# Earlier transposes for chunk 4, a new head order and a later first output step in a retention plus maxout-FFN kernel

## The chip, the cores and the metric

The kernel runs on one core of one Trainium2 chip. A time is the device time in microseconds (us) of one execution. Each kernel was executed several times, and a profile was taken of one of those executions. The profile gives every instruction's start and duration, what ended the idle time before it, and the clock that was granted to TensorE (PE). PE does the matmuls, VectorE (DVE) and ScalarE (ACT) work element by element, GpSimd (POOL) helps them, and SyncE (SP) issues nearly all the transfers. Where two kernels are compared by a ratio, they ran on the same chip in the same rounds.

## The reference

A retention layer (attention with a decaying causal mask) feeds a feed-forward layer (FFN) with a maximum over three products:

```python
B, H, S, D = 8, 8, 576, 64                      # q, k, v: float32
scores = scale * q @ k.transpose(0, 1, 3, 2)
Dmat   = where(rel >= 0, gamma[h] ** rel, 0)    # rel = query position - key position
attn   = (scores * Dmat) @ v
x = attn.transpose(0, 2, 1, 3).reshape(4608, 512)
h = maximum(maximum(x @ w1, x @ w2), x @ w3)    # w1, w2, w3: 512 x 768, float64
out = h @ w_out                                 # w_out: 768 x 512
```

## The kernel before

The rows are cut into 36 chunks of 128. Retention works chunk by chunk with a running state per head. Four chunks make one FFN tile of 512 rows, so there are nine tiles. The retention of tile t+1 is interleaved with the FFN of tile t. Only tile 0 has nothing to hide its four chunks behind, and it also has to convert the float64 weights ("pieces" of 128 columns) as they arrive. This change is about that start.

The order of program at the top is this. On PE, instructions run in this order, and each other engine also takes its own in the order written:

```python
    warm(6)                          # 6 identity matmuls, so that PE's clock is up
    for g in range(CPT):             # CPT = 4 chunks in a tile
        load(g)                      # k, q, v of chunk g
        ...
    load_weights(2)
    load(CPT)                        # chunk 4
    load_weights(4)
    decay_values(0); transposes(0)
    ...                              # gq on ACT's queue (see the diff)
    warm(2)
    scores(0); transposes(1); decay_values(1); state(0)
    values([0], [0])
    keep(0); scores(1); transposes(2); decay_values(2); state(1); keep(1)
    values([1], [1])
    transposes(3); decay_values(3); scores(2)
    convert(2)                       # weight piece 0 on DVE and ACT
    scores(3); state(2); keep(2)
    convert(2)
    values([2], [2])
    convert(2)                       # first half of weight piece 1
    decay_values(4)
    values([3], [3])
    keep(3)
    transposes(4)
    convert(4)
    # then tile 0's FFN, with the rest of chunk 4 inside it
```

Chunks are transposed on PE and copied out of PSUM by ACT. Chunk 4 still uses the two-buffer pool `ps_x`, whose banks the first FFN matmuls use as well:

```python
        for n, src in (("k", raws["k", g]), ("q", raws.pop(("q", g)))):
            pool, tag = (ps_r, "r") if g > CPT else (ps_x, "x")
            pt = pool.tile([P, NP, C], FP32, tag=tag, name=n + "t")
            for p in range(NP):
                nc.tensor.transpose(pt[:, p, :], pair(src, p), ident[:C, :C])
            t = both[n] = att.tile(...)
            nc.scalar.copy(t[:], pt[:])
```

The heads are laid out in the FFN's input so that block n holds head n in its upper 64 rows and, in its lower 64, a head of the other four with neighbours swapped. The weights' rows have to be loaded in that order, which takes three loads a piece:

```python
    def head(c, n):
        return NP * c + (n ^ c)                        # half c of block n; NP = 4
    ...
            for c, n in ((0, slice(0, NP)), (1, slice(0, NP, 2)), (1, slice(1, NP, 2))):
                h = slice(0, NP) if c == 0 else slice(head(c, n.start), H, 2)
                nc.sync.dma_start(blocks[half(c), n], heads[:, h])
```

`values` ends with the output step of its chunks: two DVE multiplications of PSUM by `gq`, which give the FFN's input `xT`.

## Time and profile before

| kernel before | |
|---|---|
| median of 3 runs | 799.44 us (799.01 to 800.44) |
| profiled execution: span, mean clock | 798.8 us, 0.998 |
| PE busy | 787.9 us |
| first FFN matmul starts | 29.12 us |
| span less that start | 769.7 us |

One view is to be added: SP's queue in the timeline of the kernel before (start, duration, instruction, how many in a row). SP issues loads one after the other, so the time in this queue delays every load behind it.

```profile
14.12 5.30 SPq L314 DMA_DIRECT2D bits<-in_moe_w_dram  x6
19.52 1.27 SPq L164 DMA_DIRECT2D kraw<-in_k_dram  x2
```

The first two weight pieces are six loads and hold the queue for 5.3 us. Chunk 4's k (two loads, since the chunk crosses from one batch to the next) is issued at 19.52.

### The profile page before, as it was taken

How to read it: one execution, taken by the hardware profiler on the slowest of the kernel's cores; microseconds unless marked ns; L12 is line 12 of the kernel's file. 1: busy time of each engine (PE TensorE's matmuls, PEld its weight loads, DVE VectorE, ACT ScalarE, POOL GpSimd, SP SyncE). 2: the span in 40 equal slices, each digit the busy share in tenths (PEclk: the TensorE clock that was granted, in tenths of full speed). 3: DMA queues.
4: the chain of work that ended last, by engine and by line, in shares of the span. 5: the costliest groups of instructions: out<-in, count | busy, mean ns of one | idle time of the engine just before them, and what ended most of it. 6: DMA issues, size and time to landing. Idle time of an engine off the chain costs nothing. (4 is left out here: it accounts for less than half of the span.)

```text
span 798.8 us, 13706 instructions
## 1 busy us (share of the span) xinstructions
PE 787.9 (99%) x5128; PEld 643.5 (81%) x5128; DVE 415.2 (52%) x833; ACT 174.4 (22%) x402; POOL 140.1 (18%) x158
## 2 busy tenths in 40 slices
PE   8899999999999999999999999999999999999998
PEld 6545546888888888888888888888888888888887
DVE  2997978664354634363535344544545343642341
ACT  3654642111111102111111111111111121111211
POOL 2210107421210130112211121112111201110000
PEclk9999999999999999999999999999999999999999
DMA  9995643333333332332233333333333323001001
GB/s 214 225 229 119 162 107 101 56 57 58 88 57 56 57 78 49 75 59 60 61 55 57 65 84 57 55 58 89 58 56 57 78 56 64 1 14 41 1 1 53
DMA packets 237506, 59.27 MB, mean 74 GB/s; under 512 B 218240, under 2 KB 236160, under 8 KB 237440
## 3 DMA queue, kind: packets, MB, share of 16 engines
q1 hardware_dynamic: 236720, 58.14, 33.5%
q8 instruction: 40, 0.66, 0.4%
q10 hardware_dynamic: 720, 0.27, 0.1%
q14 instruction: 26, 0.21, 0.1%
HBM read 48.89 MB, written 9.44 MB: 73 GB/s over the span
## 5 line engine op out<-in xcount | busy, mean ns | idle before, releaser
L498 PE MATMUL x<-S,T 128*128 128x256 f32 x576 | 148.2, 380 | 1.2 <-ACT p L503 1.2
L498 PEld LDWEIGHTS x<-S,T 128*128 128x128 f32 x576 | 108.8, 190 | 17.7 <-ACT p L503 2.8
L348 POOL TENSOR_TENSOR H<-h 128x256 f32<-128x256 f32 x24 | 21.0, 874 | 321.5 <-DVE h L541 321.5
L498 PE MATMUL x<-xT,w 128*128 128x256 f32 x288 | 76.1, 387 | 0.0
L498 PE MATMUL x<-S,w 128*128 128x256 f32 x288 | 74.4, 381 | 0.4 <-DVE h L528 0.4
L498 PE MATMUL z<-xT,T 128*128 128x256 f32 x288 | 74.0, 379 | 0.0
L498 PE MATMUL y<-xT,w 128*128 128x256 f32 x288 | 73.9, 379 | 0.0
L498 PE MATMUL z<-S,w 128*128 128x256 f32 x288 | 73.9, 379 | 0.0
L528 DVE TENSOR_TENSOR tmp<-x,p 128x256 f32<-128x256 f32 x48 | 20.4, 425 | 100.2 <-PE x L498 100.2
L269 DVE TENSOR_TENSOR xT<-o,gq 128x512 f32<-128x512 f32 (+1 forms) x40 | 23.7, 632 | 87.7 <-PE o L262 84.0
L503 ACT COPY p<-x 128x256 f32<-128x256 f32 x72 | 26.9, 373 | 191.7 <-PE x L498 191.7
L560 PE MATMUL up<-xT,w 128*128 128x512 f32 x144 | 65.2, 609 | 2.6 <-ACT kT L188 2.6
L498 PEld LDWEIGHTS z<-xT,T 128*128 128x128 f32 x288 | 54.2, 189 | 8.2 <-ACT p L503 0.3
L498 PEld LDWEIGHTS y<-xT,w 128*128 128x128 f32 x288 | 54.7, 190 | 7.4
L498 PEld LDWEIGHTS z<-S,w 128*128 128x128 f32 x288 | 54.7, 190 | 7.4
L498 PEld LDWEIGHTS x<-xT,w 128*128 128x128 f32 x288 | 53.0, 190 | 9.6 <-issue 1.5
L498 PEld LDWEIGHTS x<-S,w 128*128 128x128 f32 x288 | 49.4, 189 | 13.8 <-issue 1.3
L560 PEld LDWEIGHTS up<-xT,w 128*128 128x128 f32 x144 | 27.4, 194 | 35.5 <-issue 30.2
L227 POOL TENSOR_TENSOR state<-state,gs 128x256 f32<-128x256 f32 x24 | 20.1, 837 | 179.2 <-DVE state L226 179.2
L199 DVE TENSOR_TENSOR st<-s,causal 128x512 f32<-128x512 f32 x72 | 45.0, 684 | 11.6 <-PE s L196 10.7
L168 POOL TENSOR_TENSOR vd<-vraw,gk 128x512 f32<-128x512 f32 x36 | 38.6, 1074 | 64.8 <-DMA vraw<-in_v_dram 64.8
L503 ACT COPY u<-x 128x256 f32<-128x256 f32 x72 | 26.8, 373 | 99.5 <-PE x L498 88.6
(93 smaller groups left out, 1086.0 us busy)
## 6 DMA issues: line engine op xcount, KB each, us to landing
out_dram<-osb SPq DMA_DIRECT2D x35, 256.0 KB, 2.1
kraw<-in_k_dram SPq DMA_DIRECT2D x32, 256.0 KB, 3.1
vraw<-in_v_dram SPq DMA_DIRECT2D x32, 256.0 KB, 3.5
qraw<-in_q_dram SPq DMA_DIRECT2D x464, 16.0 KB, 1.9
kxraw<-in_k_dram SPq DMA_DIRECT2D x464, 16.0 KB, 1.9
bits<-in_moe_w_dram SPq DMA_DIRECT2D x18, 256.0 KB, 4.4
bits<-in_moe_w_dram SPq DMA_DIRECT2D x36, 128.0 KB, 4.2
bits<-in_moe_w_out_dram SPq DMA_DIRECT2D x6, 512.0 KB, 4.9
```

The costliest lines, as they stand in the source:

```text
L168: nc.gpsimd.tensor_tensor(t[:], raws.pop(("v", g))[:], gk[:].unsqueeze(2).to_broadcast([C, H, D]), op=ALU.mult)
L199: nc.vector.tensor_tensor(st[:, j], s[j][:], masks[start_of(g)][:].unsqueeze(1).to_broadcast([C, NP, C]), op=ALU.mult)
L227: nc.gpsimd.tensor_tensor(t[:], t[:], gs[:], op=ALU.mult)
L269: nc.vector.tensor_tensor(xT[t][:, b::2, i * C:(i + len(chunks)) * C].rearrange("p u (m c) -> p u m c", c=C), o[b][:].rearrange("p m u c - ...
L348: chores.append(lambda: (pool(s3, a11, a21, op=ALU.subtract), pool(s4, a12, s2, op=ALU.subtract)))
L498: nc.tensor.matmul(out[:], lhsT=w[:, d * P:(d + 1) * P], rhs=xS[t][n][:, d, :], start=first and d == 0, stop=d == 1, skip_group_check=True)
L503: nc.scalar.copy(c[:], src[:])
L528: nc.vector.tensor_tensor(c22, x[:], p7[:], op=ALU.add)
L560: nc.tensor.matmul(ps[:], lhsT=w_sb[i, fb][:, dc * P:(dc + 1) * P], rhs=xT[t][:, dc, :], start=(dc == 0), stop=(dc == NDC - 1))
```

## The change

Its intent is to take chunk 4's transposes out of the gap before the first FFN matmul, and to shorten what comes before. There are five parts:

1. `transposes(4)` moves ahead of the second weight piece and of chunk 3's values, and takes its PSUM buffers from the four-buffer pool `ps_r`.
2. Head 4c + n goes to half c of block n, so that a weight piece takes two loads instead of three, and `gq` two instead of four. The tiles of the state product now come in another order.
3. Chunk 0's output step runs after chunk 1's scores.
4. Two of six warm-up matmuls become 24 quarter-array ones (a matmul is two instructions here, so 4 instructions become 48).
5. The state update at the end of `values` now comes after the code that sums `xT` for later tiles, as a result of splitting the function.

```diff
-    gq = const.tile([P, NP, C], FP32, name="gq")
+    gq = const.tile([P, 2, NP // 2, C], FP32, name="gq")
@@
+    def warm_quarters(n):
+        ps = [ps_y.tile([P, P // 2], FP32, tag="y", name="warm") for _ in range(2)]
+        for _ in range(n):
+            for r in range(2):
+                rows = ident[P // 2 * r:P // 2 * (r + 1), :P // 2]
+                for c in range(2):
+                    nc.tensor.matmul(ps[r][P // 2 * c:P // 2 * (c + 1), :], lhsT=rows, rhs=rows, start=True, stop=True)
@@ transposes
-            pool, tag = (ps_r, "r") if g > CPT else (ps_x, "x")
+            pool, tag = (ps_r, "r") if g >= CPT else (ps_x, "x")
@@ head
-        return NP * c + (n ^ c)
+        return NP * c + n
@@ values: its end becomes a function of its own
+        finish = partial(output, chunks, o, t, i)
+        if later:
+            return finish
+        finish()
+        for g in new_states[:1]:
+            if g >= CPT:
+                keep(g)
+
+    def output(chunks, o, t, i):
         if i == 0:
             xT[t] = xpool.tile([P, NDC, NT], FP32, tag="xT", name="xT")
         ...
-        for g in new_states[:1]:
-            if g >= CPT:
-                keep(g)
         ... (sums of xT for tiles after the first)
@@ load_weights
-                for c, n in ((0, slice(0, NP)), (1, slice(0, NP, 2)), (1, slice(1, NP, 2))):
-                    h = slice(0, NP) if c == 0 else slice(head(c, n.start), H, 2)
-                    nc.sync.dma_start(blocks[half(c), n], heads[:, h])
+                for c in range(2):
+                    nc.sync.dma_start(blocks[half(c)], heads[:, head(c, 0):head(c, NP)])
@@ top
-    warm(6)
+    warm(4)
+    warm_quarters(6)
@@
-        for b in range(2):
-            nc.scalar.dma_start(gq[half(c), b::2, :], out_decay[half(b ^ c), NP // 2 * c:NP // 2 * (c + 1), :])
+        of_rows = out_decay[:, NP // 2 * c:NP // 2 * (c + 1), :].rearrange("(b p) u c -> p b (u c)", b=2)
+        nc.scalar.dma_start(gq[half(c)].rearrange("p b u c -> p b (u c)"), of_rows)
@@
-    values([0], [0])
+    first_output = values([0], [0], later=True)
     keep(0)
     scores(1)
+    first_output()
@@
     values([2], [2])
+    transposes(4)
     convert(2)
     decay_values(4)
     values([3], [3])
     keep(3)
-    transposes(4)
     convert(4)
```

(The changed reading of `gq` in the output step is cut.)

## The prediction

> **What bounds the kernel now.** I read the page first, then the timeline of each engine over the first 45 us, then the windows view, then the waits.
>
> The page's busy table says that TensorE (PE) fills the span:
>
> ```profile
> PE 787.9 (99%) x5128; PEld 643.5 (81%) x5128; DVE 415.2 (52%) x833; ACT 174.4 (22%) x402; POOL 140.1 (18%) x158
> ```
>
> The chain that ended last contains nothing but matmuls back to about 724 us, and the windows view has PE busy for all of 30 to 100 us and of 150 to 300 us. So after the first large matmul the run is a fixed queue of matmuls, and the change can only act on when that queue starts, how fast it runs, and the cost of the attention matmuls in it. Of the span less busy time, 798.8 - 787.9 = 10.9 us, 1.44 is before the first matmul and about 2.9 after the last one (795.9). About 4 us more lies between 5 and 30 us, where this change works. The PE timeline there (start, duration, instruction, in brackets the idle time before it and what ended it):
>
> ```profile
> 22.91 1.42 PE L249 MATMUL o<-st,vd 128*64 128x128 f32 x15
> ...
> 24.87 0.67 PE L262 MATMUL o<-qT,state 64*64 64x128 f32 x16
> 25.47 0.66 PE L186 MATMUL kt<-ident,kraw 128*128 128x128 f32 x4
> 25.96 0.60 PE L186 MATMUL qt<-ident,qraw 128*128 128x128 f32 x4
> 29.12 8.83 PE L560 MATMUL up<-xT,w 128*128 128x512 f32 x16 [2.56 <-ACT kT L188]
> ...
> 47.43 7.03 PE L560 MATMUL up<-xT,w 128*128 128x512 f32 x16
> ```
>
> PE finishes chunk 4's transposes at 26.56, idles 2.56 us, then starts the feed-forward. Its first 16 matmuls take 8.83 us where the same 16 take 7.03 us at 47 us: 1.80 us lost. The windows view (busy per engine, then PEclk, the DMA share, GB/s) shows why:
>
> ```profile
> 26.29:29.70 3.41, 0.85 (x5) 0.37 (x4) 3.41 (x8) 2.40 (x4) 1.57 (x2) 1.00 0.81 226
> 29.70:33.11 3.41, 3.41 (x6) 1.33 (x5) 3.38 (x8) 1.74 (x3) 0.75 (x1) 0.50 0.94 254
> ```
>
> The clock is 0.50 for exactly 3.41 us, after 3.41 us in which PE was busy 0.85. Half of 3.41 is 1.7 us, which agrees with the 1.80. So the gap costs 2.56 us of idleness and 1.8 us of clock.
>
> What ended the gap was ACT's copy of chunk 4's kT out of the bank that the first feed-forward matmul reuses. ACT could not make it earlier, since its FIFO had the second weight piece's activations first, and those wait for DVE:
>
> ```profile
> 27.12 0.72 ACT L437 ACTIVATE expo<-expo,top 128x512 f32<-128x512 int32 x1 [2.95 <-DVE expo L434]
> 27.88 0.72 ACT L440 ACTIVATE expo<-expo,inf 128x512 int32<-128x512 f32 x1
> 28.50 0.56 ACT L188 COPY kT<-kt 128x512 f32<-128x512 f32 x1
> ```
>
> DVE is the second limit. It has no idle time from 19.95 to 37.7 us:
>
> ```profile
> 19.95 1.29 DVE L199 TENSOR_TENSOR st<-s,causal 128x512 f32<-128x512 f32 x2 [2.07 <-PE s L196]
> 21.33 0.43 DVE L434 TENSOR_SCALAR expo<-bits 128x512 int32<-128x512 int32 x1
> ...
> 27.00 1.27 DVE L439 TENSOR_SCALAR frac<-bits 128x512 int32<-128x512 int32 x1
> 28.19 0.74 DVE L269 TENSOR_TENSOR xT<-o,gq 128x256 f32<-128x256 f32 x2
> ...
> 31.04 0.69 DVE L456 TENSOR_TENSOR w<-mant,expo 128x512 f32<-128x512 f32 x1
> ```
>
> The line at 28.19 is chunk 3's output step, whose first half ends near 28.6; the first feed-forward matmul needs it. So the kT copy (ends 29.06) hides a second wait only 0.4 to 0.5 us shorter.
>
> **What the Trainium skill says.** (1) "TensorE: Matmul & The Clock Gate", Part 1: PE's clock passes half its pulses after an idle window and all after a busy one; the window is about 3.4 us and free-running. The trace agrees on the 3.41 us and the half rate. It differs on the trigger: a gap of 2.56 us, shorter than a window, was enough, with PE busy 0.85 of 3.41. (2) Same page, Part 3: matmuls in different row and column tiles of the array run side by side. The trace agrees: 32 of the 64x64 tiles (L262, N=128) take 1.03 us from their start at 119.89 to the next group's at 120.92, 32 ns each, against some 107 for a whole-array instruction of that N (0.43 us at N=512, over 4). (3) "SBUF — State Buffer", Who interferes with whom: DVE's two-input and two-port instructions and GpSimd block one another. The trace agrees: the frac above took 1.27 us beside a GpSimd multiply at 26.77, and 0.42 elsewhere. (4) "DMA: Bandwidth & Descriptors", Issuing engines are not separate DMA queues: several issuers only save issue time. Here issue time is itself something: three loads per weight piece take 0.65 us each on SP where nothing blocks them.
>
> **The change, part by part.**
>
> *Chunk 4's transposes* move ahead of the second piece and of chunk 3's values, into the four-bank pool. ACT copies kT and qT before it takes up the second piece, and the first feed-forward matmul's bank was read long ago. The wait that remains is DVE's chunk 3 output; DVE's own order does not change, so its first half still ends near 28.6. Direct gain: 29.12 - 28.65 = 0.45 us.
>
> The rest of the gap is filled by moving chunk 3's values (about 2.5 us: 22.91 to 25.47) behind the transposes. These need k4 and q4, which SP issues from 19.52 to 22.15 now. I expect kt at 23 and qt at about 24.2, hence values 3 from 24.7 to 27.0, and a gap of 28.4 - 27.0 = 1.4 us in place of 2.56. The window from 26.29 would then be busy 0.7 + 1.3 = 2.0 of 3.41, 58%. It throttled at 25%; it did not in the windows from 9.23 (2.46 busy, 72%) and 12.64 (81%). I give 75% that the clock stays up, a gain of 1.75 us.
>
> *Head order 4c + n.* Loads per weight piece go from 3 to 2, those of gq from 4 to 2. In the timeline six piece loads sit between 14.12 and 19.42 on SP, 0.88 us each, ahead of chunk 4's loads; two fewer bring k4, q4 and v4 some 1.3 to 1.8 us forward, which is what makes the transposes possible at 23 us. The bytes are the same and the DMA share is near 1.0 until 17 us, so q3 (18.2) and the first piece's bits (21.3), which start DVE's chain, move little: estimate 0.3 us earlier. On ACT, gq's issue takes 4.12 us (6.04 to 10.16) and holds back kT of chunk 1; half of that goes. But chunk 3's q, on which PE waits until 18.20, absorbs it.
>
> On PE the tiles of L262 now come as r0c0, r0c1, r1c0, r1c1 and each bank gets one row half. Column pairs of the same rows already overlap (L249: 32 in 1.79 us, 56 ns each, half of 107), and so do row pairs (L196: 32 in 1.98 us). L262 is at 32 ns, a quarter of 107 plus a fixed 0.16 us per group, so there is nothing to win there: 0.
>
> *Chunk 0's output later.* DVE waited 2.58 and 1.16 us for gq and held back chunk 1's mask. That wait now lies behind chunk 1's scores. Chunk 1 comes about 1.5 us earlier and runs into the same wait for q3: 0.
>
> *Warm-up.* Four full matmuls fewer (4 instructions, 0.24 us each at the cold clock) and 24 quarter tiles more (48 instructions). At four abreast, N=64, cold, an estimate is 48 x 107 / 4 = 1.3 us plus a drain. So chunk 0 starts perhaps 0.5 us later, which the slack of about 2 us before q3 takes up: 0.
>
> Sum: 0.45 + 0.3 + 0.75 x 1.75 = 2.1 us; with a little for loads that arrive better than I assume, 2.4.
>
> Does it carry to the end? The closest pieces in the first feed-forward: the second is ready at 31.73 and its matmul would start at 28.4 + 3.43 = 31.8 (tight, perhaps 0.1 lost); later pieces are ready 2.5 us or more before use, and DVE idles for PE at 39, 51, 55 and 66 us, so it moves with PE. Yes, nearly all.
>
> **Rivals.** (a) *The clock still falls*: the free-running window may lie otherwise, and a gap of 1.4 us may be enough. Then only 0.5 to 0.9 us comes: 798.6. Chance a quarter. (b) *DVE becomes the bound*: v4 lands earlier, so GpSimd's multiply meets another DVE instruction and may lengthen the chain by up to 0.8 us; the tight second piece would wait too. About 798. (c) *q4 comes late*: since PE is in order, transposes ahead of values 3 hold those back past 28 us; then the new wait is for q4: 799 to 800. The early issue speaks against it. (d) *The new tile order loses overlap*: at two abreast L262 would gain 0.43 us per 16, over 448/16 = 28 groups 12 us: 810. The overlap of column pairs seen in L249 speaks against it: 4%. (e) *The transfers come earlier than I think* and DVE's chain with them: 795.5.
>
> **Range and chances.** From the median 799.44, less 2.4: 797.0. The runs before spread over 1.4 us, and the clock is worth 1.8; so 795.3 to 799.2. Two per cent is 16 us, which nothing in the first 30 us can give. Slower by 2% needs (d) and more: 0.02; faster: 0.01.
>
> **What would show it.** First feed-forward matmul at 28.0 to 28.7, released by DVE's xT of L269 and no longer by ACT; PEclk 1.00 from 30 to 33 and 16 such matmuls in 7.0 us; kt and qt of chunk 4 ahead of the last values; SP's k4 issue near 18; L262 still near 32 ns. I am wrong if the clock still dips, if PE waits for q4, or if L262's busy time grows.

## The result, and the profile after

| | before | after |
|---|---|---|
| median | 799.77 us (799.01 to 800.44, 4 runs) | 798.75 us (797.69 to 799.21, 4 runs) |
| span and clock of the profiled execution | 798.8 us, 0.998 | 796.0 us, 1.000 |
| first FFN matmul starts | 29.12 us | 28.75 us |

The ratio of after to before is 0.9986, with a 95% interval of 0.9968 to 1.0003: the same within 2%, and about 1.1 us less. Here and below a ratio is the mean time of one kernel's fast runs over the mean time of the other's fast runs of the same rounds. That is not quite the ratio of the medians quoted.

The profiled execution of after was its luckiest. It was the 797.69 one, and its clock stayed at 1.000. The other three had 0.997 or 0.998 and took 798.53 to 799.21 us. So the traces show 2.8 us between the kernels where the medians show 1.0.

The busy table of after:

```profile
PE 785.0 (99%) x5172; PEld 643.0 (81%) x5172; DVE 417.6 (52%) x833; ACT 174.4 (22%) x402; POOL 139.9 (18%) x158
```

PE has 44 instructions more (48 of quarter matmuls for 4 of full ones) and is busy 2.9 us less, though the work is the same. Most of that is clock: 1.7 us in the first 16 FFN matmuls, as the next view shows. PE's timeline of after (start, duration, instruction, in brackets the idle time before it and what ended it):

```profile
21.26 0.67 PE L270 MATMUL o<-qT,state 64*64 64x128 f32 x16
24.67 0.63 PE L194 MATMUL kt<-ident,kraw 128*128 128x128 f32 x4 [2.74 <-DMA kraw<-in_k_dram]
25.52 0.63 PE L194 MATMUL qt<-ident,qraw 128*128 128x128 f32 x4 [0.22 <-issue]
26.08 1.09 PE L257 MATMUL o<-st,vd 128*64 128x128 f32 x16
...
27.57 0.67 PE L270 MATMUL o<-qT,state 64*64 64x128 f32 x16
28.75 7.13 PE L573 MATMUL up<-xT,w 128*128 128x512 f32 x16 [0.51 <-DVE xT L286]
```

The gap in front of the FFN has shrunk from 2.56 to 0.51 us, and its releaser is now DVE instead of ACT. But a new gap of 2.74 us has opened four us earlier, where the transposes wait for chunk 4's k. The FFN starts 0.37 us earlier. Its first 16 matmuls now last 7.06 us from their start to the next group's (28.75 to 35.81), where before had 8.76 (29.12 to 37.88). The two add up to 0.37 + 1.70 = 2.07 us at that point. The difference stays there, at 2.04 to 2.07 us, up to about 479 us. The trace of before then shows a few more stalls of 0.2 to 0.45 us each, which have no counterpart in the change.

What DVE and ACT did at the same place in after (two answers of the timeline, one for each engine):

```profile
28.27 0.76 DVE L286 TENSOR_TENSOR xT<-o,gq 128x256 f32<-128x256 f32 x2 [1.05 <-PE o L270]
```

```profile
25.34 0.59 ACT L196 COPY kT<-kt 128x512 f32<-128x512 f32 x1 [2.04 <-PE kt L194]
```

ACT's copy is now over long before the FFN. DVE, which had no idle time here before, waits 1.05 us for PE to finish chunk 3's values. So the order of waits is now: transfer of k4, then PE, then DVE, then the FFN. DVE was ready for chunk 3's output at 27.22, earlier than before (28.19), mostly since its instruction at L452 took 0.42 us, where the same one (L439 before) took 1.27 us beside a GpSimd multiply.

SP's queue of after in the timeline:

```profile
14.81 3.03 SPq L327 DMA_DIRECT2D bits<-in_moe_w_dram  x4
17.93 1.27 SPq L172 DMA_DIRECT2D kraw<-in_k_dram  x2
...
21.25 3.08 SPq L172 DMA_DIRECT2D vraw<-in_v_dram  x2
```

k4 is issued 1.59 us earlier than before, as intended. It still lands only at about 24.6, some 6.7 us after its issue.

The new tile order of the state product costs and gains nothing. The groups by form, first before, then after (instructions, then total busy us, mean ns of one, idle before):

```profile
L262 PE MATMUL o<-qT,state 64*64 64x128 f32 x448 | 16.7, 277 | 0.0
```

```profile
L270 PE MATMUL o<-qT,state 64*64 64x128 f32 x448 | 16.7, 277 | 0.0
```

### The profile page after: what moved, and what is told of

Its sections match the earlier page's. It is cut to its first block, busy times and chain, and to the rows that moved or that the text cites. A ratio compares the mean times of both kernels' runs of the same rounds, so it can differ in the third digit from the quotient of the medians.

```text
span 796.0 us, 13774 instructions
## 1 busy us (share of the span) xinstructions
PE 785.0 (99%) x5172; PEld 643.0 (81%) x5172; DVE 417.6 (52%) x833; ACT 174.4 (22%) x402; POOL 139.9 (18%) x158
## 4 chain that ended last, share of the span: by engine, by line
PE 95%; SPq 2%; DMA 1%; issue 0%; ACT 0%; DVE 0%; ACTq 0%
PE x L511 32%; PE z L511 15%; PE dx L383 11%; PE up L573 8%; PE y L511 8%; PE dz L383 5%; PE s L204 4%; PE o L257 4%; PE dy L383 3%; PE down L562 2%; PE o L270 2%; PE kv L224 2%; SPq L172 1%; DMA kraw<-in_k_dram 1%; SPq L327 0%; DMA out_dram<-osb 0%
## 5 line engine op out<-in xcount | busy, mean ns | idle before, releaser
L573 PE MATMUL up<-xT,w 128*128 128x512 f32 x144 | 63.5, 596 | 0.5 <-DVE xT L286 0.5
L383 PE MATMUL dx<-To,H 128*128 128x256 f32 x192 | 44.8, 383 | 0.0
```

Of the source, the lines that this page charges most:

```text
L383: nc.tensor.matmul(out[m], lhsT=hS[n](fp)[:, m * P:(m + 1) * P], rhs=late["T"][n][:, fp, :], start=first and fp == 0 and (m == 0 or last a ...
L573: nc.tensor.matmul(ps[:], lhsT=w_sb[i, fb][:, dc * P:(dc + 1) * P], rhs=xT[t][:, dc, :], start=(dc == 0), stop=(dc == NDC - 1))
```

## The experiments

Twelve kernels were run. A name with `a_` is the kernel after with an edit, one with `b_` the kernel before with an edit. Each was timed in five rounds against the kernel before. "Start" is the start of the first FFN matmul in its trace, "rest" is the span less that start, and "clock kept" counts the runs with a mean clock of 0.999 or more.

| kernel | median us (range) | ratio to before [95%] | start | rest | clock kept |
|---|---|---|---|---|---|
| a_same | 798.14 (796.97–799.80) | 0.9981 [0.9964, 0.9997] | 28.70 | 767.2 | 3 of 6 |
| a_fill | 797.71 (797.30–797.85) | 0.9972 [0.9957, 0.9986] | 28.91 | 767.2 | 5 of 5 |
| b_fill | 798.24 (797.44–800.94) | 0.9987 [0.9969, 1.0005] | 28.96 | 767.1 | 4 of 6 |
| b_transposes | 799.65 (797.65–801.44) | 0.9998 [0.9980, 1.0017] | 27.90 | 768.6 | 3 of 6 |
| b_trans_quarters | 800.05 (798.56–802.30) | 1.0004 [0.9990, 1.0017] | 28.90 | 769.6 | 4 of 6 |
| a_old_heads | 800.01 (798.22–803.20) | 1.0004 [0.9982, 1.0027] | 30.25 | 768.7 | 2 of 6 |
| a_full_warm | 797.88 (796.40–799.05) | 0.9975 [0.9963, 0.9987] | 29.80 | 767.2 | 2 of 5 |
| a_output_first | 798.32 (797.03–799.06) | 0.9976 [0.9961, 0.9991] | 30.08 | 767.2 | 3 of 6 |
| a_k4_early | 796.68 (795.08–797.05) | 0.9956 [0.9943, 0.9969] | 27.74 | 767.3 | 5 of 5 |
| a_k4_osb4 | 797.33 (796.70–797.81) | 0.9965 [0.9951, 0.9980] | 27.89 | 767.3 | 3 of 5 |
| a_k4_osb4_full | 797.29 (796.51–798.59) | 0.9966 [0.9952, 0.9980] | 29.18 | 767.6 | 1 of 6 |
| a_k4_fill | 796.50 (796.32–797.17) | 0.9956 [0.9940, 0.9972] | 26.58 | 768.0 | 6 of 6 |

The kernel before had medians of 799.69 to 800.05. The column "rest" already says much: in seven of the twelve, and in the first profile of after (767.2), it is 767.1 to 767.3, whatever the start. From the first FFN matmul on, the run is a fixed queue. The five others are taken up below.

### The kernel after once more: how much of its gain is the clock

> The changed kernel again, unedited, to see whether its runs fall into two groups. Theory (the granted clock falls or not according to where the free-running 3.4 us window lies against PE's gap of 2.74 us before chunk 4's transposes): runs with a mean clock of 1.000 end near 797.6 us, runs with 0.997 or 0.998 near 799.0 us, about 1.7 us apart. Rival (the spread is noise from elsewhere): times don't follow the clock. Median expected 798.7, ratio to before 0.9985.

This is the unedited kernel after. With the four runs of the first result there are ten runs of it, and 44 of the kernel before from these experiments, so here not all runs are of the same rounds. Sorted by the mean clock of the run:

| | clock 0.999 or more | 0.998 or less | mean of all |
|---|---|---|---|
| before | 5 of 44 runs, mean 798.47 us | 39 runs, mean 800.15 us | 799.96 us |
| after | 4 of 10 runs, mean 797.41 us | 6 runs, mean 799.15 us | 798.45 us |

In either column after is 1.0 to 1.06 us shorter, and in either row a run with a fallen clock is about 1.7 us longer (1.68 and 1.74). The whole difference is 1.50 us. It is the 1.0 us at the same clock, and (39/44 - 6/10) x 1.7 = 0.49 us from falling less often. Ten runs are few to know that share.

### Dummy matmuls in the wait of the kernel after

```diff
+    def fill(n, pool=None, tag="y"):
+        ps = (pool or ps_y).tile([P, P], FP32, tag=tag, name="fillps")
+        for _ in range(n):
+            nc.tensor.matmul(ps[:], lhsT=ident[:], rhs=ident[:], start=True, stop=True)
@@
     values([2], [2])
+    fill(12, ps_x, "x")
     transposes(4)
```

> The changed kernel with 12 idle-time matmuls of the identity (24 instructions, some 2.6 us) put into PE's wait for chunk 4's k, in a bank that nothing else uses then. Theory (the clock): every run keeps a mean clock of 1.000 and ends near 797.5 us, 1.2 us under the median of the changed kernel. Rival (the time is in the wait for k4, or in noise): no change against a_same, clock still 0.997 to 0.998 in some runs.

PE's timeline of this kernel, two groups of it:

```profile
22.15 2.94 PE L134 MATMUL fillps<-ident 128*128 128x128 f32 x24
...
28.91 7.13 PE L578 MATMUL up<-xT,w 128*128 128x512 f32 x16 [0.51 <-DVE xT L291]
```

The dummies lie exactly in the wait for k4 and end about when it has landed. All five runs kept their clock, and they spread over 0.55 us, where the unedited kernel spread over 2.8. The start is no earlier than in the unedited one (28.91 against 28.70), so the whole effect is the clock. As far as five runs can show it, the new wait for k4 is where the kernel after loses its clock.

### The same in the kernel before

```diff
     transposes(4)
+    fill(10)
     convert(4)
```

> The kernel before with 10 idle-time matmuls of the identity (20 instructions, some 2.1 us) in its gap of 2.56 us ahead of the first feed-forward matmul; the wait for ACT's copy of kT stays. Theory (1.8 of the 2.06 us between the two traces are the clock, 0.37 the earlier start): 1.7 us faster than before, near 798.0 us, clock 1.000. Rival (the wait for the copy is what costs): same as before, 799.7.

The profiled run has the first FFN matmul at 28.96 and 16 of them in the time of full clock (7.07 us), and a rest of 767.1. Four of six runs took 797.44 to 798.51. Two took 800.39 and 800.94 at a clock of 0.998, and no trace was taken of those. The profiled run agrees with the account of where the old kernel's 1.7 us went. The whole set is inconclusive: its interval includes 1, and what lowered the clock in two runs isn't known.

### The transposes alone

```diff
-            pool, tag = (ps_r, "r") if g > CPT else (ps_x, "x")
+            pool, tag = (ps_r, "r") if g >= CPT else (ps_x, "x")
@@
     values([2], [2])
+    transposes(4)
     convert(2)
@@
     keep(3)
-    transposes(4)
     convert(4)
```

> The kernel before with only chunk 4's transposes moved ahead and into the other banks; head order, loads and warm-up as before. Theory (PE is in order, so the transposes hold chunk 3's values until k4 and q4 land, and without the earlier issue of the loads these land near 25.5 us): values 3 after 26 us, first feed-forward matmul at 28.7 to 29.5 us, so no earlier start than in the changed kernel, and a gap ahead of the transposes in which the clock can still fall: 799.0 to 800.0 us. Rival (the move alone carries the gain): 798.7.

PE's timeline of this kernel:

```profile
23.29 0.63 PE L186 MATMUL kt<-ident,kraw 128*128 128x128 f32 x4 [0.98 <-DMA kraw<-in_k_dram]
...
27.90 7.13 PE L560 MATMUL up<-xT,w 128*128 128x512 f32 x16 [1.16 <-DVE xT L269]
```

Here the expectation of the start was a miss on the good side. k4 came at 23.3, although the old head order was kept and k4 was issued at 18.70, after that of the kernel after (17.93). The FFN starts 1.2 us before that of the kernel before. Yet the median is no better than before's (ratio 0.9998), and the rest is 768.6 instead of 767.2. In this trace something further on takes the gain away. The trace shows PE waiting 2.20 us at 129 us, where before waits 0.89. That is followed up below.

### The transposes with the quarter warm-up

```diff
-    warm(6)
+    warm(4)
+    warm_quarters(6)
```

(on top of the last edit)

> The kernel before with the moved transposes and the quarter tiles, but the old head order, loads and output order. Theory H1 (instruction fetches moved by the quarter tiles): kt of chunk 4 moves from 23.3 us to 24.5 us or later, first feed-forward matmul near 28.7 us. Rival H2 (weight or gq loads): kt stays near 23.3 us, first feed-forward matmul near 27.9 us.

PE's timeline of this kernel, the transposes and the place near 131 us:

```profile
24.38 0.63 PE L195 MATMUL kt<-ident,kraw 128*128 128x128 f32 x4 [1.75 <-DMA kraw<-in_k_dram]
...
131.06 1.13 PE L507 MATMUL x<-S,T 128*128 128x256 f32 x4 [3.19 <-ACT p L512]
```

k4 is late again, at 24.38. The median is 800.05, and PE now waits 3.19 us near 131.

### The old head order in the kernel after

```diff
-        return NP * c + n
+        return NP * c + (n ^ c)
@@
-                for c in range(2):
-                    nc.sync.dma_start(blocks[half(c)], heads[:, head(c, 0):head(c, NP)])
+                for c, n in ((0, slice(0, NP)), (1, slice(0, NP, 2)), (1, slice(1, NP, 2))):
+                    h = slice(0, NP) if c == 0 else slice(head(c, n.start), H, 2)
+                    nc.sync.dma_start(blocks[half(c), n], heads[:, h])
```

(and `gq` in four loads)

> The changed kernel with the old head order, hence three loads per weight piece and four for gq. Theory (SP's queue of loads sets when the first feed-forward's outputs are stored at 124 us: with 18 more loads of 0.65 us SP comes to the stores 1 to 1.5 us after the data, ACT's copies wait for their two buffers, and PE waits 2 to 3 us near 129 us in place of 1.3): first feed-forward matmul at 28.7 to 29.3 us, but median 799.3 to 800.0 us, 1 to 2 us over the changed kernel. Rival (the head order matters only in the first 30 us): PE's waits between 100 and 140 us stay at 1.3 us, median 798.0 to 798.7.

Near 125 us tile 0's FFN is done, and its results have to leave: ACT copies them into two buffers, and SP stores them. SP's, ACT's and PE's timelines of this kernel there, one answer each:

```profile
126.55 0.53 SPq L172 DMA_DIRECT2D vraw<-in_v_dram  x1
127.17 5.08 SPq L568 DMA_DIRECT2D out_dram<-osb  x4
```

```profile
124.95 0.58 ACT L567 COPY osb<-down 128x512 f32<-128x512 f32 x1 [12.29 <-PE down L563]
...
130.71 1.19 ACT L567 COPY osb<-down 128x512 f32<-128x512 f32 x2 [4.32 <-DMA out_dram<-osb]
```

```profile
132.23 1.13 PE L512 MATMUL x<-S,T 128*128 128x256 f32 x4 [3.01 <-ACT p L517]
```

ACT's first copy ends at 125.53. The store of it is issued only at 127.17, since SP is still issuing loads until 127.1. Both buffers are then full, ACT waits 4.32 us, and the copy `p` that PE needs stands behind it in ACT's queue. The same in the unedited run of the kernel after:

```profile
120.19 0.51 SPq L172 DMA_DIRECT2D vraw<-in_v_dram  x1
124.02 4.36 SPq L567 DMA_DIRECT2D out_dram<-osb  x4
```

```profile
128.34 1.13 PE L511 MATMUL x<-S,T 128*128 128x256 f32 x4 [0.67 <-ACT p L516]
```

With 18 loads fewer, SP has issued the last load 3.8 us ahead of the store, which goes out as soon as ACT's first copy is done, and PE waits 0.67 us. In this trace a second loss is mixed in: the clock fell once, from 14.46 to 17.87, and the FFN started at 30.25. The claim about the stores rests on the waits near 130, not on the median.

SP's last load before those stores, and PE's waits between 100 and 140 us for ACT's p and DVE's h:

| kernel | last load issued | first store issued | first copy begun | PE waits |
|---|---|---|---|---|
| before | 124.92 | 126.13 | 125.52 | 1.3 us |
| b_fill | 122.44 | 124.28 | 123.67 | 1.3 us |
| b_transposes | 123.44 | 124.06 | 122.61 | 2.2 us |
| b_trans_quarters | 124.95 | 125.58 | 123.61 | 3.2 us |
| a_old_heads | 126.55 | 127.17 | 124.95 | 3.0 us |
| a_same | 120.19 | 124.02 | 123.41 | 1.3 us |

Before was just in time: its FFN was so late that SP kept up. In b_transposes, b_trans_quarters and a_old_heads the first copy begins earlier, SP with the old number of loads comes late, and PE gives the gain back. In the trace of b_transposes that is where the gain of the transposes went.

b_fill is the exception. It has the old loads too, and its first copy begins at 123.67, as in b_trans_quarters (123.61). Yet SP has issued its last load 2.5 us earlier, and PE waits 1.3 us. So the old number of loads makes SP late in three of these traces, but not in every execution with an early FFN. Why SP was ahead in b_fill was not followed. The runs that kept their clock point the same way: 798.48 us on average for b_transposes (3 runs) and 799.68 for b_trans_quarters (4), but 797.93 for b_fill (4), and 797.41 for the kernel after. The extra wait (0.9, 1.9 and 1.7 us over 1.3) in the three late traces covers most of their excess in "rest" over 767.2 (1.4, 2.4 and 1.5 us). For the kernel before, the excess is 2.5 us, of which 1.7 is the clock and 0.8 is left, in which the small stalls named above lie.

### The full warm-up in the kernel after

```diff
-    warm(4)
-    warm_quarters(6)
+    warm(6)
```

> The changed kernel with the old warm-up (six full matmuls, no quarter tiles). In three traces of the changed kernel and its filled copy chunk 4's k arrives at 24.65 to 24.9 us, in the trace of the kernel before plus the moved transposes at 23.3 us. Theory H1: the quarter tiles add 88 instructions to PE's queue, so that PE's own instruction fetches (16 KB each on queue 8) fall at 10.8 and 20.9 us in place of 15 and 23 to 25 us, beside the loads of chunks 2 and 4, and hold these up: without the quarters kt of chunk 4 starts near 23.3 us, the first feed-forward matmul near 27.9 us, 0.8 us less time than the changed kernel. Rival H2: the larger weight loads or gq's loads ahead of k4 delay it: kt stays near 24.7 us and the time near 798.2 us.

The prediction of k4 at 23.3 failed: it came at 24.38, after a wait of 3.31 us. In this trace the clock fell, which the windows view shows (stretch, length, busy time with instruction counts for PE, PEld, DVE, ACT and POOL, then clock, DMA share, GB/s):

```profile
22.17:25.58 3.41, 1.20 (x10) 0.88 (x10) 3.38 (x7) 0.53 (x1) 1.10 (x1) 1.00 0.60 146
25.58:28.99 3.41, 3.41 (x46) 3.29 (x48) 0.45 (x2) 3.07 (x6) 1.04 (x1) 0.50 0.98 252
```

PE busy for 1.20 of 3.41 us (35%) was followed by half the clock for exactly 3.41 us. What ran in that window was chunk 3's values, ahead of the FFN, so the FFN started at 29.80. The median, 797.88, is close to the unedited kernel's. The quarter matmuls neither gain nor cost anything that these rounds can show.

### Chunk 0's output step at its old place

```diff
-    first_output = values([0], [0], later=True)
+    values([0], [0])
     keep(0)
     scores(1)
-    first_output()
```

> The changed kernel with chunk 0's output step back ahead of chunk 1's scores. Theory (chunk 1's slack ahead of chunk 3's q absorbs it): first feed-forward matmul unchanged at 28.7 us give or take 0.5, median within 0.6 us of 798.2. Rival (gq's wait holds DVE and so chunk 1, 2 and 3): start over 0.8 us later, median near 799.2.

The median is 798.32 against 798.14 for the unedited kernel; the two ranges lie over each other. The late start in its trace (30.08) comes from a fallen clock, at 25.00. The part is neutral.

### k4 ahead of the second weight piece

```diff
-    def load(g):
+    def load(g, names="kqv"):
     ...
+            if n not in names:
+                continue
@@
+    load_weights(1)
+    load(CPT, "kq")
     load_weights(2)
-    load(CPT)
-    load_weights(4)
+    load(CPT, "v")
+    load_weights(3)
```

> The changed kernel with the loads of chunk 4's k and q ahead of the second weight piece and its v behind the third. Theory (what bounds the start now is k4's landing, then DVE's chain): kt of chunk 4 near 22.5 us, no PE gap over 1 us between 21.9 and the first feed-forward matmul, which starts at 27.5 to 28.0 us; the clock stays at 1.00 and the runs lie close together near 796.7 us, 1.4 us under the median of the changed kernel. Rival (the second piece, now 0.5 MB later, becomes the wait): the second group of eight feed-forward matmuls waits for its weights, start at 28.7 us or no gain: 798.0 us.

PE's timeline of this kernel:

```profile
23.42 0.63 PE L196 MATMUL kt<-ident,kraw 128*128 128x128 f32 x4 [0.57 <-DMA kraw<-in_k_dram]
24.37 0.63 PE L196 MATMUL qt<-ident,qraw 128*128 128x128 f32 x4 [0.33 <-DMA qraw<-in_q_dram]
...
27.74 7.13 PE L575 MATMUL up<-xT,w 128*128 128x512 f32 x16 [0.65 <-DVE xT L288]
```

With k4 and q4 ahead of one weight piece, the wait falls from 2.74 to 0.57 us, the start moves to 27.74, and the rest stays at 767.3. All five runs kept their clock. The median is 796.68, ahead of both kernels. So the wait for k4 did bound the start in the kernel after.

### Four output buffers, with and without the full warm-up

```diff
-    opool = ctx.enter_context(tc.tile_pool(name="opool", bufs=2))
+    opool = ctx.enter_context(tc.tile_pool(name="opool", bufs=4))
```

(on top of the last edit; the second kernel has `warm(6)` as well)

> The changed kernel with chunk 4's k and q loaded ahead of the second weight piece (as a_k4_early, 796.7) and four in place of two output buffers. Theory (the 0.6 to 0.7 us that PE waits near 128 us is ACT's copy behind the stores of two output buffers): that wait goes, the one for DVE near 132 us stays or grows by up to 0.7: median 796.0 to 796.7. Rival (DVE's chain sets both waits): 796.7.

> The same as a_k4_osb4 with the old warm-up of six full matmuls in place of the quarter tiles. Theory (in the trace of a_full_warm the early chunks run about 1 us earlier without the quarter tiles, and k4 is no longer what PE waits for): first feed-forward matmul at 26.7 to 27.2 us in place of 27.7, median 795.3 to 796.0. Rival (the loads set the start all the same): start at 27.7, same time as a_k4_osb4.

ACT no longer waits for stores. In exchange, PE waits 1.58 us for DVE's h at 131.89, where the unedited kernel waits about 0.6 for it, and the rest is 767.3 as with two buffers. The wait has moved to DVE, as the rival had it, and nothing is gained. The median, 797.33, is above both forecasts. Two of its five runs lost the clock, where a_k4_early, with the same start, lost it in none of five, so five runs are few to judge that share. The second kernel missed its expectation. k4 was transposed at 22.17, but q4 came at 24.40, the clock fell, and the start was 29.18.

### All waits of PE filled

```diff
+    fill(5, ps_x, "x")
     transposes(2)
@@
+    fill(2, ps_x, "x")
     transposes(4)
@@
     keep(3)
+    fill(2, ps_x, "x")
     convert(4)
```

(on top of the early k4)

> The changed kernel with chunk 4's k and q loaded ahead of the second weight piece, and idle-time matmuls of the identity in the three places where PE still waits (5 ahead of chunk 2's transposes, 2 ahead of chunk 4's, 2 ahead of the first feed-forward matmul). In the twelve traces that record clock events the clock fell after a 3.41 us window with PE busy 52% or less and never after one with 56% or more. Theory: with no window under 60% every run keeps the clock, and the runs lie within 1 us of each other near 796.5 us. Rival (the 2 us spread of a_k4_early comes from the loads and from the waits near 130 us): spread as there, median 796.7, or later by up to 0.5 us where a fill outlasts its wait.

PE's timeline of this kernel:

```profile
26.58 7.54 PE L580 MATMUL up<-xT,w 128*128 128x512 f32 x16 [0.63 <-DVE xT L293]
```

This is the best version: a median of 796.50, all six runs at 0.999 or more, within 0.85 us. Its ratio, 0.9956, is that of the early k4 without dummies. The start is 1.16 us earlier, which can hardly be the dummies' doing: in this execution the loads landed earlier from chunk 2 on (its k is transposed at 12.77 us, where a_k4_early waited for it until 13.83). But the first 16 matmuls take 0.4 us more. The trace has DVE finish the second weight piece at 30.37, and PE, at the pace of the other kernels, would have taken it up at about 30.1. So the start has run into the weights, which gives back 0.4 of the 1.16 us. The rest is 768.0, and the other 0.4 above 767.2 was not traced. The same 7.54 us in place of 7.13 stand in the trace of a_k4_osb4_full, which explains its rest of 767.6.

### What lowers the clock

The clock events in the traces that record them (that of after records none), by PE's busy share in the 3.41 us window before. The borders of the windows are counted from the first event of each trace, in steps of 3.413 us:

| busy in the window before | followed by |
|---|---|
| in the first 40 us: 25% (before), 26% (a_output_first), 35% (a_full_warm), 40% (a_k4_osb4_full), 52% (a_old_heads) | half clock, for 3.41 us |
| in the first 40 us: 56% (b_trans_quarters), 57% (a_same), 59% (a_output_first), 60% (a_k4_osb4), 62% (a_old_heads), more | full clock |
| near 130 us: 46% (b_trans_quarters), 50% (a_old_heads), 54% (a_k4_osb4), 55% (a_k4_osb4_full), more | full clock |

The windows view of a_old_heads and of b_trans_quarters, the nearest cases of the first 40 us on either side, and then b_trans_quarters near 130 us:

```profile
11.04:14.46 3.42, 1.76 (x26) 1.35 (x23) 1.85 (x4) 0.75 (x2) 0.00 (x0) 1.00 0.81 188
14.46:17.87 3.41, 3.41 (x32) 2.79 (x32) 1.04 (x3) 1.17 (x2) 1.11 (x2) 0.50 0.93 211
```

```profile
23.41:26.82 3.41, 1.92 (x22) 1.57 (x24) 3.38 (x7) 1.52 (x4) 1.11 (x1) 1.00 0.85 197
26.82:30.23 3.41, 2.75 (x43) 1.79 (x40) 3.41 (x8) 2.64 (x4) 1.90 (x2) 1.00 0.93 257
```

```profile
129.22:132.63 3.41, 1.57 (x7) 1.42 (x8) 3.05 (x7) 1.82 (x4) 2.69 (x5) 1.00 0.44 162
132.63:136.05 3.42, 3.42 (x17) 2.92 (x17) 1.79 (x5) 0.74 (x2) 2.40 (x3) 1.00 0.22 34
```

In the first 40 us the busy share separates the two outcomes. Over the whole run it doesn't: near 130 us a window of 46% kept the clock, where one of 52% lost it at 11 us. So the share of time in which PE is busy is not all that counts. The matmuls in the windows near 130 us use the whole array (128*128), most of those in the window at 11 us half of it (64*128, 128*64). Whether that is the reason is not shown.

The windows lie differently in each execution. A wait of 2.52 us lay within one window in a_output_first and cost the clock. One of the same length was cut by a border, at 23.61, in a_same and didn't. This fits that one kernel has two groups of times, but only the profiled executions could be looked at.

### What stays open

- Why k4, issued at 17.9 in the kernel after, lands at 24.6, while in b_transposes, issued at 18.7, it lands at 23.3. In the traces with a late k4, transfers of the instruction queue (16 KB each, 0.9 to 1.8 us) lie among the loads at 18.5 to 21.9 us. In b_transposes the nearest lies at 25.3. That is a correlation. The theory that the quarter matmuls shift them foresaw b_trans_quarters (24.38) but not a_full_warm (24.38 as well), and so isn't settled.
- The 1.0 us between the kernels at the same clock. The start accounts for 0.4. In the one trace of the kernel before, 0.8 us of its rest is neither clock nor a wait near 130, and it has no trace at full clock.
- What besides PE's busy share decides whether the clock falls, and why SP's loads were issued in time in b_fill.
- Part 5 of the change, the order of the state update, was not isolated.
- b_fill's two slow runs.

## Why the prediction was right or wrong

The prediction was right in its class and its range: the measured median, 798.75 us, lies within 795.3 to 799.2, though 1.75 us above the 797.0 given.

- **What bounds the kernel: right.** The rest after the first FFN matmul is 767.1 to 767.3 us in the eight traces without an excess, whose starts lie between 27.7 and 30.1 us.
- **Direct gain of 0.45 us, and DVE's output as the next releaser: right, but the size in part by luck.** The start moved by 0.37 us, released by DVE. The prediction had DVE's own order hold that output near 28.2. Instead DVE was ready at 27.22 and then waited 1.05 us for PE, whose values k4 had held back, so that the output came at 28.27. The further 0.3 us from earlier loads did not come at the start.
- **"I expect kt at 23 and qt at about 24.2": wrong in size.** kt came at 24.67 and qt at 25.52. SP's issue near 18 was foreseen rightly, but not the 6.7 us to landing. The values of chunk 3 therefore ended at 28.2, not 27.0. The gap before the FFN is 0.51 us rather than 1.4, but the idle time went in front of the transposes instead. The early k4 (23.42, start 27.74) shows that this was the term that held the start back.
- **"75% that the clock stays up": too high.** Four of ten runs of the kernel after kept it. The prediction looked at the window after 26.3, but the risk was now in the wait for k4 a few us earlier. And before was taken as always throttled, while 5 of 44 runs were not. The clock's term, 1.3 us in the sum, came to 0.49 us. The 1.75 us that a fall costs was right: 1.70 in the traces, 1.68 and 1.74 between the groups of runs.
- **Rival (a), the clock still falls: happened in six of ten runs**, at 799.15 us against its 798.6. **Rival (c), q4 late: happened in another form.** The transfer was k4, and the values ended at 28.2 us, early enough for the start to gain a little still. **Rivals (b) and (e)** didn't happen: DVE waited for PE, and the transfers came later. **Rival (d)** is refuted by the 277 ns in both kernels.
- **"Chunk 0's output later: 0" and the warm-up's 0: right** within the rounds (798.32 and 797.88 against 798.14). The "four full matmuls fewer" are two, in four instructions.
- **"Does it carry to the end? Nearly all": right, for a reason it didn't have.** It named weights and DVE as what could take the gain back, and not SP's queue. In the three traces with the old loads and SP late, the gain was lost near 130 us (ratios 0.9998, 1.0004 and 1.0004); b_fill's trace lost nothing there. The new head order was credited only with bringing k4 forward; on this evidence its larger worth was 18 loads fewer ahead of the first stores.

## What to carry to other kernels

Before work is moved ahead of a wait, ask when its own data land, since the wait may only move with it; then order the loads by first use. Where PE must wait about 2.5 us or more, try dummy matmuls that end when the data come. They delayed the start by 0.2 us at most here. The clock stayed up in all 11 runs of a_fill and a_k4_fill, though only in four of six of b_fill. A fall cost 1.7 us here and made most of the spread between runs. Count what the issuing queue holds in front of a store, since a start that comes earlier can turn a queue that was just in time into the next bound.

## What the Trainium skill lacked or had wrong

- "TensorE: Matmul & The Clock Gate", Part 1 has the clock fall after an idle window of about 3.4 us, and the page's closing table warns of PE-idle gaps over about 3 us. It also tells that frequent short idling makes the clock swing, but gives no share. Here a single gap of 2.56 us was enough, and so were gaps of 0.39 and 1.27 us in one window (a_old_heads). In the first 40 us windows in which PE was busy 52% or less lost the clock and those with 56% or more kept it, but near 130 us windows of 46 to 55% kept it as well. Its window length and free running agree: each fall lasted 3.41 us, and the same kernel fell in some runs and not in others.
- The same page, Part 4, says that transposes do not count as PE work for the clock in the same way. Here they may count: they stand as matmuls against the identity in the trace, and with them the windows of the first 40 us separate at 52 and 56%. Left out, they do not: the window of a_old_heads that lost the clock would be busy 46%, that of b_trans_quarters that kept it 19% (1.92 less twice 0.63 us, over 3.41). Since the windows near 130 us don't follow the busy share, this is a hint and not shown.
- "DMA: Bandwidth & Descriptors", Issuing engines are not separate DMA queues, calls the sequencer's issue time usually small relative to the transfer. For one load that holds: a weight load held SP for 0.65 us where nothing blocked it, whether of 128 or 256 KB, and landed after 4.2 to 5.4 us (medians). But eighteen such loads make 11.7 us (worked out), and in the three traces in which they made the stores late PE waited 0.9 to 1.9 us longer.
- No page read has what transfers of the instruction queue do to loads beside them. The traces show them at 16 KB and 0.9 to 2.2 us each, 40 or 41 in a run; their effect is open.
